# Lightning attention followed by a gated feed-forward: the five sums of w_out's quarters in tiles of their own, all formed by GpSimd, and the last products in column halves

## The chip, the cores and the metric

The kernel runs on 1 core of one Trainium2 chip. The metric is the device time of one execution in microseconds (us), lower is better. Times of a kernel are given as the median of several runs; a profile is one further execution, with its own time.

## The reference

Attention with a decay per head over blocks of 64 positions (batch 4, 8 heads, 768 positions, 64 channels), and then a feed-forward layer of 3072 tokens x 512 with a width of 2048 whose gate is h * cos(h):

```python
for b in range(nb):                      # 12 blocks of 64
    intra = np.einsum('bhic,bhjc->bhij', qb, kb) * Dmask[None]
    intra = np.einsum('bhij,bhjd->bhid', intra, vb)
    inter = np.einsum('bhid,bhde->bhie', qb * lam_pow[None], kv_state)
    out[:, :, sl] = intra + inter
    kb_dec = kb * rev_pow[None]
    kv_state = lam_block[None, :, None, None] * kv_state + np.einsum('bhsd,bhse->bhde', kb_dec, vb)
...
x = attn_out.transpose(0, 2, 1, 3).reshape(B * S, H * D)   # 3072 x 512
h = x @ w_in                             # 512 x 2048
g = h * np.cos(h)
return (g @ w_out).astype(np.float32)    # 2048 x 512
```

## The kernel before, in words

**Blocks and tiles.** The 3072 tokens are 24 blocks of 128 (n = 0 to 23), handled in pairs (pair p holds blocks 2p and 2p+1). The first two pairs ("spans") have code of their own at the start of the kernel (`add_span`). The feed-forward takes the blocks in nine tiles of 4, 2, 2, 2, 2, 4, 2, 2, 4 blocks (`TILES`, L32).

**Attention per pair.** `prepare` (L355) loads q, k and v of a pair over SP's DMA queue, scales q (L369) and v (L377) and casts k (L373), from pair 3 on all six on GpSimd, and from pair 3 on has q and k transposed by DMAs that SP issues (L405) into qkT. The loads of the next pair's q, k and v stand behind these two transposes on SP's queue. `add_scores` and `add_stretch` hold TensorE's part: scores (L447), the update of the state (L459), values (L509, L541); VectorE masks the scores (L452) and adds up the state (L465); ScalarE copies the outputs into xT (L549), the feed-forward's input.

**Feed-forward, plain tiles (0 to 4), `add_ffn`.** Hidden products (L1001), cosine on ScalarE (L1007), gate on VectorE (L1013), output products with w_out (L1048), copies and stores. The outputs of blocks 0 to 11 are held in the ring o_held until pair 10's transposes are issued, and stored by L1072 and L1074.

**Feed-forward, fast tiles (5 to 8, `FAST`), `add_fast_ffn`.** The product with w_out is done for two blocks at a time by one Strassen step: g is split by blocks and halves of the width, w_out into quarters 11, 12, 21, 22 (halves of its 2048 rows by halves of its 512 columns), and seven products replace eight. They need sums of g's parts, formed by VectorE per tile (L850, L852, L853, bf16), and five sums of w_out's quarters, formed once (`add_w_sums`, L776). The products (L897, numbered "1" to "7") go into PSUM banks A, B, C, for the last pair of blocks also D. ScalarE copies bank A (L914), VectorE forms the differences E (L921) and the outputs (L931 or L932, L958 or L959), which SP and, for the last piece, ScalarE's queue store (L948, L949, L964, L966).

**The five sums before.** 11+22, 12-22 and 21-11 (`WIDE`) are formed by GpSimd into three tiles of the ring "wide" (3 buffers), which before that hold s_m_sp0, s_m_sp1 and v_sp of the spans. Each is made in four instructions of 128x512 elements. Each of these twelve depends on the scaling of one block's v, from block 6 to block 17 (`SLOT`, L37), so that two stand in GpSimd's stream per pair. 21+22 and 11+12 are formed by VectorE, in eight instructions, in place: they overwrite the quarters 21 and 12 of w_out itself, so they also wait for the last output product of the plain tiles (`closed`) and for the GpSimd sums that read the same quarters.

**What sets the order.** All work is given as tasks with an engine, a duration, dependencies and a priority to a planner (`Planner.order`, L87). It simulates the engines in time, starts on each the task of lowest priority number among those that can start first, and the instructions are emitted in the order of the plan. Rings of buffers (`BUFS`) and the 8 PSUM banks are part of the simulation; a task with `lock` (VectorE's sums) and GpSimd's tasks are not planned at the same time. `SEQ` (L39) fixes the order of the products within a pair of blocks: for the last pair of blocks "5234176", each in two groups g of four of the eight slices of the width.

**The last pair of blocks.** Products "7" and then "6" are the last 16 instructions of TensorE (L897, 256 columns each). VectorE adds E to "7" (first L959), then to "6" (second L959); SP stores the first, ScalarE's queue the second.

Of the kernel before, what the change touches and what calls it, by code (L numbers as in the profile page):

```python
# [10 lines left out]
F32 = mybir.dt.float32  # L11
BF16 = mybir.dt.bfloat16
# [6 lines left out]
SPANS = 2  # L19
# [12 lines left out]
TILES = [4, 2, 2, 2, 2, 4, 2, 2, 4]  # L32
WIDE = ["11+22", "12-22", "21-11"]
CMB = (-4.0, 1.0, 6.0)
HASTE = 10.0
ON = ["DDDDDDDDDD"] * 9
SLOT = list(range(6, 18))  # L37
WSUM = [("11+22", "POOL", 2, 70.0), ("12-22", "POOL", 2, 70.0), ("21-11", "POOL", 2, 70.0), ("21+22", "DVE", 2, 100.0), ("11+12", "DVE", 2, 100.0)]
SEQ = [[(n, (g,)) for g, x in enumerate(("52341", "34521")) for n in x] + [(n, (0, 1)) for n in "76"], [(n, (0, 1)) for n in "5234176"]]  # L39
# [130 lines left out]
def kernel(  # L170
# [10 lines left out]
    nc = tc.nc  # L181
    B, H, S, D = q.shape
    P = 128
    NB = S // P
    NBLK = B * NB
    NP = H // 2
# [13 lines left out]

    BUFS = {"ld": 4, "qk": 3, "v_s": 6, "qkT": 3, "s_m": 4, "cos": 3, "o_held": 13, "cmb": 6, "SA": 1, "E": 1}
    ctx.enter_context(tc.manual_schedule())
# [6 lines left out]
    def bank(i, shape, dt, name):  # L209
# [405 lines left out]
    spans, span_deps = [], []  # L615
    span_s = [consts.tile([P, 2, NP, 2, P], BF16, tag="wide", bufs=3, name=f"s_m_sp{x}") for x in range(SPANS)]
    span_vs = consts.tile([P, SPANS, H, 2, D], BF16, tag="wide", bufs=3, name="v_sp")
    span_v = [span_vs[:, x] for x in range(SPANS)]
# [138 lines left out]

    W, w_sum, passed, closed = {}, {}, {}, [None]
# [12 lines left out]

# [19 lines left out]

    def right(what, f):
        a, z = what[:2], what[3:]
        if z:
            if what in WIDE:
                return W[what][:, f]
            return w_out_sb[:, f, high] if what == "11+12" else w_out_sb[:, HF + f, low]
        return w_out_sb[:, f + (HF if a[0] == "2" else 0), low if a[1] == "1" else high]

    def add_fast_ffn(i):  # L800
# [75 lines left out]
        for p in range(np_):  # L876
# [9 lines left out]
            for name, gs in SEQ[min(p, 1)]:  # L886
                to, half = where_[name]
                what = plan_of[name][2]
                for g in gs:
                    k += 1  # L890
                    opens = opening.get(name) if name not in count else None

                    def product(task, name=name, g=g, p=p, to=to, half=half, what=what, opens=opens):
# [3 lines left out]
                        return [nc.tensor.matmul(t, lhsT=left(name, f, p), rhs=right(what, f),  # L897
                                                 start=(f % QF == 0 and opens is not None), stop=(f == HF - 1), skip_group_check=True)
                                for f in range(QF * g, QF * g + QF)]
# [4 lines left out]
                    t.many = True  # L904
                    before = done[name] = t
                    count[name] = count.get(name, 0) + 1
# [45 lines left out]

            def second_out(_, half, cut=None, p=p):
                if ("o2", i, p) not in live:
                    live["o2", i, p] = work.tile([P, 2, HM], F32, tag="o_held", bufs=BUFS["o_held"], name="o_sb")
                o, e = live["o2", i, p], live["E", i, p]
                if half is None:
                    return nc.vector.tensor_add(o, live["f", i, p, "C"], e)  # L958
                return nc.vector.tensor_add(o[:, half], live["f", i, p, "CD"[half]][:, half], e[:, half])  # L959

            def store_second(_, half, p=p, rows=rows):
                o = live["o2", i, p]
                if half != 0:
                    nc.sync.dma_start(out=out[rows(0), low], in_=o[:, 1])  # L964
                if half != 1:
                    (nc.scalar if half == 0 else nc.sync).dma_start(out=out[rows(1), high], in_=o[:, 0])  # L966

            if last:
                x = pl.add("DVE", DUR["half"][0], [done["7"], done["e"]], partial(second_out, half=1), at(1.0), get="o_held", lat=DUR["half"][1])
                y = pl.add("DVE", DUR["half"][0], [done["6"], x], partial(second_out, half=0), at(1.0), lat=DUR["half"][1])  # L970
                x.frees = [dma("SP", 0.6, 0.7, partial(store_second, half=1), n0 + 2 * p + 9, [x], ordered=False)[1],
                           dma("ACT", 0.6, 0.7, partial(store_second, half=0), n0 + 2 * p + 9, [y], ordered=False)[1]]
                heads["C"].bank_frees, heads["D"].bank_frees = [[y]], [[x]]
                e0.frees = [x, y]
            else:
                x = pl.add("DVE", DUR["gate"][0], [done["7"], done["6"], done["e"]], partial(second_out, half=None), at(1.0), get="o_held", lat=DUR["gate"][1])
                x.frees = [dma("SP", 0.95, 1.3, partial(store_second, half=None), n0 + 2 * p + 9, [x], ordered=False)[1]]
                heads["C"].bank_frees = [[x]]
                e0.frees = [x]
# [3 lines left out]
    def add_ffn(i):  # L983
# [48 lines left out]
        for j in range(nb):  # L1032
# [5 lines left out]
            for piece, part in enumerate(pieces):  # L1038
# [21 lines left out]
                o_last[i] = store  # L1060
                closed[0] = store

# [158 lines left out]
```

## Time and profile before

| what | value |
|---|---|
| median of 3 runs | 200.58 us (200.28 to 203.41) |
| profiled execution, own time | 200.86 us |
| span of the profiled execution | 199.2 us |
| granted TensorE clock, mean | 0.999 |
| mean of a GpSimd sum of quarters (128x512, bf16) | 1.15 us, 12 of them |
| VectorE sums of quarters (128x512, bf16) | 0.41 to 1.07 us, 8 of them, 109.4 to 119.3 us after the start |

The engines are named PE (TensorE; PEld is its weight loads), DVE (VectorE), ACT (ScalarE), POOL (GpSimd) and SP (SyncE, which issues DMAs). In a row in order of time the first number is the start in us from the beginning of the span, the second the length; a row may hold several like instructions (x count); in brackets at its end stands the idle time of the engine ahead of it and who ended it. "issue" as the cause means that the profile shows nothing that the engine waited for. Busy times are modelled for matmuls, whose ends overlap, so a single product reads longer than the distance to the next.

### The profile page before, as it was taken

To read this page: it belongs to the slowest core of one execution; us is meant where nothing else is said; L and a number is where in the kernel's file an instruction comes from. 1 tells how busy PE (TensorE), PEld (TensorE's weight loads), DVE (VectorE), ACT (ScalarE), POOL (GpSimd) and SP (SyncE) were. 2 spreads that over 40 slices of the span, in tenths; PEclk is the share of its full clock that TensorE was granted. 3 is DMA by queue.
4 is the path that set the end of the run, shared out by engine and by line. 5 is a ranking of instruction groups with operands and counts; after the bars stand their busy time and mean duration, and the time that the engine had idled before them with its cause. 6 is when DMAs were issued, how large, how long until landed. Compare 5 with 4: busy or idle time off the path is not lost.

```text
span 199.2 us, 6216 instructions
## 1 busy us (share of the span) xinstructions
PE 190.0 (95%) x2577; PEld 130.1 (65%) x2599; DVE 146.3 (73%) x284; ACT 113.7 (57%) x217; POOL 79.3 (40%) x98
## 2 busy tenths in 40 slices
PE   8999999999999999999999998999799999999993
PEld 3577444658748647858655444778788885656882
DVE  2978772448857816957755899999797898599933
ACT  4888771329778636929564886544434565565110
POOL 5893002285856766778687373001640000000000
PEclk9999999999999999999999999999999999999999
DMA  5999999989999989899999999798991011001133
GB/s 161 306 190 203 206 203 240 318 192 159 248 188 170 216 175 221 166 255 149 250 188 285 186 238 125 174 379 240 226 177 56 3 54 56 0 4 49 56 105 107
DMA packets 98254, 34.48 MB, mean 173 GB/s; under 512 B 84914, under 2 KB 96178, under 8 KB 98226
## 3 DMA queue, kind: packets, MB, share of 16 engines
q1 hardware_dynamic: 91248, 29.76, 69.5%
q0 software_dynamic: 6832, 4.20, 14.5%
q8 instruction: 20, 0.33, 0.7%
q10 hardware_dynamic: 146, 0.13, 0.2%
q14 instruction: 8, 0.07, 0.1%
HBM read 27.26 MB, written 6.29 MB: 168 GB/s over the span
## 4 chain that ended last, share of the span: by engine, by line
PE 87%; DVE 7%; DMA 2%; issue 2%; ACT 1%; DVEq 0%
PE ps_h L1001 21%; PE ps_f L1048 21%; PE ps_h L820 17%; PE ps_f L897 17%; DVE g L829 3%; DMA sp_f<-in_q_dram 2%; DVE cmb L850 2%; PE ps_o L509 2%; PE ps_t L642 1%; PE ps_o L541 1%; PE ps_kv L459 1%; PE ps_s L447 1%; PE ps_s L653 1%; PE ps_o L679 1%; PE ps_idle L1143 1%
## 5 line engine op out<-in xcount | busy, mean ns | idle before, releaser
L826 ACT ACTIVATE cos<-ps_h,halfpi 128x512 f32<-128x512 f32 x48 | 32.9, 688 | 26.4 <-PE ps_h L820 24.9
L820 PE MATMUL ps_h<-xT,w_in_sb 128*128 128x256 bf16 (+1 forms) x251 | 46.6, 325 | 1.2 <-DVE g L829 0.9
L1013 DVE TENSOR_TENSOR g<-ps_h,cos 128x256 bf16<-128x256 f32 (+1 forms) x85 | 37.8, 459 | 12.2 <-ACT cos L1007 10.8
L1048 PE MATMUL ps_f<-w_out_sb,g 128*128 128x512 bf16 x177 | 42.3, 379 | 1.7 <-issue 1.3
L1001 PE MATMUL ps_h<-xT,w_in_sb 128*128 128x256 bf16 (+1 forms) x338 | 43.5, 286 | 0.1
L1007 ACT ACTIVATE cos<-ps_h,halfpi 128x256 f32<-128x256 f32 (+1 forms) x85 | 39.1, 505 | 7.1 <-PE ps_h L1001 6.9
L1001 PEld LDWEIGHTS <-w_in_sb 128*128 128x128 bf16 x340 | 33.0, 98 | 10.4 <-DMA w_in_sb<-in_moe_w_in_dram 0.3
L369 POOL TENSOR_TENSOR qk<-q_f,q_scale 128x512 bf16<-128x512 f32 x19 | 20.0, 1070 | 40.9 <-DMA q_f<-in_q_dram 37.5
L829 DVE TENSOR_TENSOR g<-ps_h,cos 128x512 bf16<-128x512 f32 x48 | 32.1, 685 | 5.3 <-ACT cos L826 5.2
L820 PEld LDWEIGHTS <-w_in_sb 128*128 128x128 bf16 x256 | 24.9, 98 | 14.4 <-DVE g L829 1.0
L1048 PEld LDWEIGHTS <-g 128*128 128x128 bf16 x192 | 18.0, 98 | 18.7
L377 POOL TENSOR_TENSOR v_s<-v_f,v_scale 128x512 bf16<-128x512 f32 x19 | 20.1, 1057 | 13.9 <-DMA v_f<-in_v_dram 11.8
L897 PEld LDWEIGHTS <-g 128*128 128x128 bf16 x192 | 18.6, 98 | 4.0
L549 ACT CAST xT<-ps_o 128x512 bf16<-128x512 f32 x15 | 8.1, 589 | 15.0 <-PE ps_o L541 12.6
L897 PEld LDWEIGHTS <-cmb 128*128 128x128 bf16 x144 | 14.0, 98 | 3.8 <-DVE cmb L850 0.7
L452 DVE TENSOR_TENSOR s_m<-ps_s,mask 128x512 bf16<-128x512 f32 x20 | 12.9, 685 | 2.8 <-PE ps_s L447 2.3
L373 POOL CAST qk<-k_f 128x512 bf16<-128x512 f32 x18 | 11.3, 625 | 7.4 <-DMA k_f<-in_k_dram 7.2
L850 DVE TENSOR_TENSOR cmb<-g 128x1024 bf16<-128x1024 bf16 (+1 forms) x24 | 13.9, 604 | 0.2
L897 PE MATMUL ps_f<-w_out_sb,cmb 128*128 128x256 bf16 x96 | 13.3, 273 | 0.4 <-DVE cmb L850 0.4
L897 PE MATMUL ps_f<-w_out_sb,g 128*128 128x256 bf16 x96 | 12.4, 273 | 0.0
L1065 ACT COPY o_sb<-ps_f 128x512 f32<-128x512 f32 x12 | 6.9, 588 | 6.9 <-PE ps_f L1048 6.9
L465 DVE TENSOR_TENSOR sum<-sum,ps_kv 128x512 f32<-128x512 f32 x15 | 10.2, 683 | 0.6
(100 smaller groups left out, 191.4 us busy)
## 6 DMA issues: line engine op xcount, KB each, us to landing
q_f<-in_q_dram SPq DMA_DIRECT2D x20, 256.0 KB, 3.5
k_f<-in_k_dram SPq DMA_DIRECT2D x20, 256.0 KB, 4.5
v_f<-in_v_dram SPq DMA_DIRECT2D x20, 256.0 KB, 5.1
out_dram<-o_sb SPq DMA_DIRECT2D x31, 128.0 KB, 2.0
out_dram<-o_sb SPq DMA_DIRECT2D x8, 256.0 KB, 3.0
w_out_sb<-in_moe_w_out_dram POOLq DMA_DIRECT2D x3, 512.0 KB, 13.6
sp_f<-in_q_dram SPq DMA_DIRECT2D x2, 512.0 KB, 4.8
sp_f<-in_k_dram SPq DMA_DIRECT2D x2, 512.0 KB, 5.4
```

Source lines behind the costliest of these rows:

```text
L369: return vec[e].tensor_mul(new_qk()[:, 0, :, s], live.pop(("q_f", 2 * pr + s)), q_scale[:, c, :].unsqueeze(2).to_broadcast([P, H, D]))
L377: return vec[e].tensor_mul(live["v_s", 2 * pr + s], live.pop(("v_f", 2 * pr + s)), v_scale[:, c, :].unsqueeze(2).to_broadcast([P, H, D]))
L452: return nc.vector.tensor_mul(t, live["s", pr][s], mask.unsqueeze(1).to_broadcast([P, H, D]))
L820: return [nc.tensor.matmul(t[:, x], lhsT=w_in_sb[:, kd, f * P:(f + 1) * P], rhs=live["xT", i][:, kd, :cols], start=(kd == 0), stop=(kd == ...
L826: return nc.scalar.activation(c, live["h", i, fs[0]], AF.Sin, bias=halfpi)
L829: return nc.vector.tensor_mul(g_tile()[:, fs[0]:fs[-1] + 1:HF, :cols], live.pop(("h", i, fs[0])), live.pop(("c", i, fs[0])))
L850: return v.tensor_add(c, *{"5": (a11, a12), "2": (a21, a22), "1": (a11, a22)}[name])
L897: return [nc.tensor.matmul(t, lhsT=left(name, f, p), rhs=right(what, f), start=(f % QF == 0 and opens is not None), stop=(f == HF - 1), sk ...
L1001: return [nc.tensor.matmul(t[:, :n], lhsT=w_in_sb[:, kd, f * P:(f + 1) * P], rhs=live["xT", i][:, kd, at], start=(kd == 0), stop=(kd == KD ...
L1007: nc.scalar.activation(c[:, :n], live["h", i, f, at.start][:, :n], AF.Sin, bias=halfpi)
L1013: return nc.vector.tensor_mul(live["g", i][:, f, at], live.pop(("h", i, f, at.start))[:, :n], live.pop(("c", i, f, at.start))[:, :n])
L1048: return [nc.tensor.matmul(live["f", i, j, piece][:, :width], lhsT=live["g", i][:, f, j * P:(j + 1) * P], rhs=w_out_sb[:, f, part], start= ...
```

## The change

It does four things.

1. All five sums get tiles of their own in the ring "wide", which grows from 3 buffers to 5, so w_out's quarters are no longer overwritten, and the waits for `closed` and for other sums are dropped.
2. All five are formed by GpSimd, in 20 instructions. The new `SLOT` ties three of them to the scalings of v in each of the pairs 3 to 8 (blocks 6, 6, 7; 8, 8, 9; and so on to 16, 16, 17) and two to block 18.
3. Room is made: qk goes from 3 buffers to 2, o_held from 13 to 12, mask_sp shares the buffer of E, kv_bd that of SA.
4. In the last pair of blocks product "6" is formed in two column halves: all eight slices of the width for columns 0 to 127, then all eight for 128 to 255, 16 products of 128 columns in place of 8 of 256. The second output is then added and stored in three parts: the 256 columns of "7" (SP), the first 128 of "6" (SP), the last 128 (ScalarE's queue).

```diff
-WIDE = ["11+22", "12-22", "21-11"]
...
-SLOT = list(range(6, 18))
-WSUM = [("11+22", "POOL", 2, 70.0), ("12-22", "POOL", 2, 70.0), ("21-11", "POOL", 2, 70.0), ("21+22", "DVE", 2, 100.0), ("11+12", "DVE", 2, 100.0)]
+SLOT = [6, 6, 7, 8, 8, 9, 10, 10, 11, 12, 12, 13, 14, 14, 15, 16, 16, 17, 18, 18]
+WSUM = [(x, "POOL", 2, 70.0) for x in ("11+22", "12-22", "21-11", "21+22", "11+12")]
...
-    BUFS = {"ld": 4, "qk": 3, "v_s": 6, "qkT": 3, "s_m": 4, "cos": 3, "o_held": 13, "cmb": 6, "SA": 1, "E": 1}
+    BUFS = {"ld": 4, "qk": 2, "v_s": 6, "qkT": 3, "s_m": 4, "cos": 3, "o_held": 12, "cmb": 6, "SA": 1, "E": 1}
...
-    mask_sp = consts.tile([P, 2, P], F32)
+    mask_sp = work.tile([P, 2, P], F32, tag="E", bufs=BUFS["E"], name="mask_sp")
...
-    kv_bd = consts.tile([P, 2, NP, P], BF16)
+    kv_bd = work.tile([P, 2, NP, P], BF16, tag="SA", bufs=BUFS["SA"], name="kv_bd")
...
         def place(name, g):
-            if name in WIDE:
-                if name not in W:
-                    W[name] = consts.tile([P, HF, HM], BF16, tag="wide", bufs=3, name=f"w_{name}")
-                return W[name][:, QF * g:QF * g + QF]
-            return w_out_sb[:, QF * g:QF * g + QF, high] if name == "11+12" else w_out_sb[:, HF + QF * g:HF + QF * g + QF, low]
+            if name not in W:
+                W[name] = consts.tile([P, HF, HM], BF16, tag="wide", bufs=5, name=f"w_{name}")
+            return W[name][:, QF * g:QF * g + QF]
...
-                    t = pl.add(e, {"DVE": 0.07 + 0.55 / parts, "POOL": 2.08 / parts}[e], loaded + slot + (wide_free if name in WIDE else [closed[0]] + w_sum[{"11+12": "12-22", "21+22": "21-11"}[name], g]),
+                    t = pl.add(e, {"DVE": 0.07 + 0.55 / parts, "POOL": 2.08 / parts}[e], loaded + slot + wide_free,
...
+                        if last and name == "6":
+                            m = slice(g * P, (g + 1) * P)
+                            return [nc.tensor.matmul(t[:, m], lhsT=left(name, f, p), rhs=right(what, f)[:, m],
+                                                     start=False, stop=(f == HF - 1), skip_group_check=True) for f in range(HF)]
...
             if last:
-                x = pl.add("DVE", DUR["half"][0], [done["7"], done["e"]], partial(second_out, half=1), at(1.0), get="o_held", lat=DUR["half"][1])
-                y = pl.add("DVE", DUR["half"][0], [done["6"], x], partial(second_out, half=0), at(1.0), lat=DUR["half"][1])
...
+                parts = [slice(HM, DM), slice(0, P), slice(P, HM)]
+                x = second(parts[0], [done["7"]], True, at(1.0))
+                y = second(parts[1], [done["6", 0], x], False, at(1.0))
+                z = second(parts[2], [done["6", 1], y], False, at(1.0))
+                x.frees = [second_store(parts[0], nc.sync, [x], 0.6), second_store(parts[1], nc.sync, [y], 0.4), second_store(parts[2], nc.scalar, [z], 0.4)]
```

`second(at, ...)` is one VectorE addition over the columns `at`, `second_store` the store of the same columns. The rest of the diff carries these through.

More of the change, by code (lines that the diff above doesn't have):

```diff
@@ L615 @@
     spans, span_deps = [], []
-    span_s = [consts.tile([P, 2, NP, 2, P], BF16, tag="wide", bufs=3, name=f"s_m_sp{x}") for x in range(SPANS)]
-    span_vs = consts.tile([P, SPANS, H, 2, D], BF16, tag="wide", bufs=3, name="v_sp")
+    span_s = [consts.tile([P, 2, NP, 2, P], BF16, tag="wide", bufs=5, name=f"s_m_sp{x}") for x in range(SPANS)]
+    span_vs = consts.tile([P, SPANS, H, 2, D], BF16, tag="wide", bufs=5, name="v_sp")
     span_v = [span_vs[:, x] for x in range(SPANS)]
@@ L756 @@
     hid, closing = [], None
-    W, w_sum, passed, closed = {}, {}, {}, [None]
+    W, w_sum, passed = {}, {}, {}
     low, high = slice(0, HM), slice(HM, DM)
@@ L794, in right @@
         if z:
-            if what in WIDE:
-                return W[what][:, f]
-            return w_out_sb[:, f, high] if what == "11+12" else w_out_sb[:, HF + f, low]
+            return W[what][:, f]
         return w_out_sb[:, f + (HF if a[0] == "2" else 0), low if a[1] == "1" else high]
@@ L891, in add_fast_ffn, with product @@
                     opens = opening.get(name) if name not in count else None
-                    def product(task, name=name, g=g, p=p, to=to, half=half, what=what, opens=opens):
+                    def product(task, name=name, g=g, p=p, to=to, half=half, what=what, opens=opens, last=last):
                         if opens:
@@ L904, in add_fast_ffn @@
                     t.many = True
-                    before = done[name] = t
+                    before = done[name] = done[name, g] = t
                     count[name] = count.get(name, 0) + 1
@@ L951, in add_fast_ffn, with second_out @@
             out1.frees = [dma("SP", 0.95, 1.3, store_first, n0 + 2 * p + 8, [done["o1", 0]], ordered=False)[1]]
-            def second_out(_, half, cut=None, p=p):
+            def second_out(_, at, p=p):
                 if ("o2", i, p) not in live:
[L955 to L959, printed above, removed]
@@ L961, in store_second @@
-            def store_second(_, half, p=p, rows=rows):
-                o = live["o2", i, p]
[L963 to L966, printed above, removed]
-            if last:
-                x = pl.add("DVE", DUR["half"][0], [done["7"], done["e"]], partial(second_out, half=1), at(1.0), get="o_held", lat=DUR["half"][1])
-                y = pl.add("DVE", DUR["half"][0], [done["6"], x], partial(second_out, half=0), at(1.0), lat=DUR["half"][1])
[L971 to L974, printed above, removed]
-            else:
-                x = pl.add("DVE", DUR["gate"][0], [done["7"], done["6"], done["e"]], partial(second_out, half=None), at(1.0), get="o_held", lat=DUR["gate"][1])
-                x.frees = [dma("SP", 0.95, 1.3, partial(store_second, half=None), n0 + 2 * p + 9, [x], ordered=False)[1]]
@@ new lines, in second_out, with store_second @@
+                    live["o2", i, p] = work.tile([P, DM], F32, tag="o_held", bufs=BUFS["o_held"], name="o_sb")
+                t = live["f", i, p, "D" if last and at.start == HM else "C"].rearrange("p a m -> p (a m)")
+                return nc.vector.tensor_add(live["o2", i, p][:, at], t[:, at], live["E", i, p].rearrange("p a m -> p (a m)")[:, at])
+            def store_second(_, at, queue, p=p, rows=rows):
+                o = live["o2", i, p]
+                if at.stop > HM:
+                    nc.sync.dma_start(out=out[rows(0), low], in_=o[:, high])
+                if at.start < HM:
+                    e = min(at.stop, HM)
+                    queue.dma_start(out=out[rows(1), HM + at.start:HM + e], in_=o[:, at.start:e])
@@ new lines, in second, with second_store @@
+            def second(at, deps, get, prio):
+                n = (at.stop - at.start) / 256.0
+                return pl.add("DVE", 0.07 + 0.265 * n, deps + [done["e"]], partial(second_out, at=at), prio, get="o_held" if get else None, lat=0.17)
+            def second_store(at, queue, deps, us):
+                return dma("SP" if queue is nc.sync else "ACT", us, 1.5 * us, partial(store_second, at=at, queue=queue), n0 + 2 * p + 9, deps, ordered=False)[1]
+            if last:
+                parts = [slice(HM, DM), slice(0, P), slice(P, HM)]
[3 more added lines that the diff above has]
+                x.frees = [second_store(parts[0], nc.sync, [x], 0.6), second_store(parts[1], nc.sync, [y], 0.4), second_store(parts[2], nc.scalar, [z], 0.4)]
+                heads["C"].bank_frees, heads["D"].bank_frees = [[z]], [[x]]
+                e0.frees = [x, y, z]
+            else:
+                x = second(slice(0, DM), [done["7"], done["6"]], True, at(1.0))
+                x.frees = [second_store(slice(0, DM), nc.sync, [x], 0.95)]
@@ L1060, in add_ffn @@
                 o_last[i] = store
-                closed[0] = store
                 def project_out(_, eng, j=j, piece=piece, width=width, tag=tag):
```

## The prediction

> **What bounds the kernel now.** I read the page first, then busy time by stretch, then each engine in order of time around the weakest stretch.
>
> ```profile
> span 199.2 us, 6216 instructions
> PE 190.0 (95%) x2577; PEld 130.1 (65%) x2599; DVE 146.3 (73%) x284; ACT 113.7 (57%) x217; POOL 79.3 (40%) x98
> ```
>
> TensorE (PE) works in 190.0 of 199.2 us, so all that an edit can win by better order is inside the other 9.2 us. Where these are is shown by busy time per stretch (columns: stretch, length, busy time and instructions of PE, weight loads, VectorE = DVE, ScalarE = ACT, GpSimd = POOL, then clock, DMA share, GB/s):
>
> ```profile
> 109.00:120.00 11.00, 10.95 (x169) 5.51 (x170) 10.28 (x19) 8.82 (x14) 6.57 (x7) 1.00 1.38 212
> 120.00:133.00 13.00, 11.61 (x96) 8.15 (x95) 12.97 (x21) 6.72 (x11) 1.17 (x2) 1.00 0.76 210
> ```
>
> From 120 to 133 TensorE misses 1.39 us and VectorE works without a break (12.97 of 13). One stretch earlier VectorE is almost as full, but TensorE misses only 0.05. TensorE in order of time shows the two places (the bracket is the idle time before, and who ended it):
>
> ```profile
> 121.19 4.49 PE L820 MATMUL ps_h<-xT,w_in_sb 128*128 128x512 bf16 x19 [0.93 <-DVE g L829]
> ...
> 132.20 0.61 PE L897 MATMUL ps_f<-w_out_sb,cmb 128*128 128x256 bf16 x4 [0.41 <-DVE cmb L850]
> ```
>
> Both waits, 0.93 + 0.41 = 1.34 us, are for VectorE. What VectorE does ahead of them, with the last ScalarE cosine of that run, the one GpSimd scaling that lies beside, and the group of the VectorE sums from the costliest groups by form:
>
> ```profile
> 109.38 1.07 DVE L776 TENSOR_TENSOR w_out_sb<-w_out_sb 128x512 bf16<-128x512 bf16 x1
> ...
> 119.35 1.05 DVE L776 TENSOR_TENSOR w_out_sb<-w_out_sb 128x512 bf16<-128x512 bf16 x1
> 120.44 1.29 DVE L829 TENSOR_TENSOR g<-ps_h,cos 128x512 bf16<-128x512 f32 x2
> 121.64 1.28 DVE L452 TENSOR_TENSOR s_m<-ps_s,mask 128x512 bf16<-128x512 f32 x2
> 122.84 1.50 DVE L850 TENSOR_TENSOR cmb<-g 128x1024 bf16<-128x1024 bf16 x1
> ...
> 131.46 1.28 DVE L850 TENSOR_TENSOR cmb<-g 128x1024 bf16<-128x1024 bf16 x2
> ```
>
> ```profile
> 118.89 0.69 ACT L826 ACTIVATE cos<-ps_h,halfpi 128x512 f32<-128x512 f32 x1 [0.18 <-PE ps_h L820]
> ```
>
> ```profile
> 122.75 1.04 POOL L377 TENSOR_TENSOR v_s<-v_f,v_scale 128x512 bf16<-128x512 f32 x1 [2.63 <-DMA v_f<-in_v_dram]
> ```
>
> ```profile
> L776 DVE TENSOR_TENSOR w_out_sb<-w_out_sb 128x512 bf16<-128x512 bf16 x8 | 4.9, 634 | 0.0
> ```
>
> The eight sums that VectorE forms stand in 109.4 to 120.4, among the gates of the first Strassen tile (tile 5), and push the last two gates to 120.44. The second of these two needs only the cosine that ends at 118.89 + 0.69 = 119.58.
>
> **The change part by part.**
>
> *Sums leave VectorE.* Eight instructions, 4.9 us, go. The last two gates then start when their cosines end, the second at about 119.6 instead of 121.0 (120.44 plus half of 1.29). VectorE is some 1.3 us earlier from there on, and the bank for which TensorE waited until 121.19 is free by 120.3, when the attention products in front are just through (121.19 - 0.93 = 120.26). Term: -0.93. The second wait, 0.41 at 132.20, ends on a row of VectorE work with no gap from 119.35 on. That row starts 1.3 us earlier and TensorE comes only 0.93 earlier, so 0.4 of it is covered; besides, the sum that took 1.50 at 122.84 beside GpSimd's scaling at 122.75 has the chance to run ahead of it. Term: -0.41. Bounds for the two: both gone, -1.34; none, because TensorE stalls at the next thing, 0.
>
> *Sums go to GpSimd.* What a sum costs there, and how GpSimd's rounds are spaced now: a round per pair of blocks is two scalings of q (L369), two casts of k, two scalings of v, with now two sums behind them; the bracket is GpSimd's idle time ahead of the round.
>
> ```profile
> 52.62 2.04 POOL L369 TENSOR_TENSOR qk<-q_f,q_scale 128x512 bf16<-128x512 f32 x2 [0.62 <-DMA q_f<-in_q_dram]
> ...
> 64.18 2.04 POOL L369 TENSOR_TENSOR qk<-q_f,q_scale 128x512 bf16<-128x512 f32 x2 [1.58 <-PE ps_h L1001]
> ...
> 75.06 2.04 POOL L369 TENSOR_TENSOR qk<-q_f,q_scale 128x512 bf16<-128x512 f32 x2 [1.68 <-PE ps_s L447]
> ...
> 85.33 2.04 POOL L369 TENSOR_TENSOR qk<-q_f,q_scale 128x512 bf16<-128x512 f32 x2 [0.32 <-DMA q_f<-in_q_dram]
> ...
> 91.08 1.16 POOL L776 TENSOR_TENSOR w_21-11_2005<-w_out_sb 128x512 bf16<-128x512 bf16 x1
> ...
> 96.11 2.04 POOL L369 TENSOR_TENSOR qk<-q_f,q_scale 128x512 bf16<-128x512 f32 x2 [1.75 <-DMA q_f<-in_q_dram]
> ...
> 105.30 2.04 POOL L369 TENSOR_TENSOR qk<-q_f,q_scale 128x512 bf16<-128x512 f32 x2 [0.86 <-DMA q_f<-in_q_dram]
> ...
> 114.78 2.10 POOL L369 TENSOR_TENSOR qk<-q_f,q_scale 128x512 bf16<-128x512 f32 x2 [2.55 <-DMA q_f<-in_q_dram]
> ```
>
> The new SLOT puts three sums instead of two behind the v's of pairs 3 to 8 (one more, 1.15 us each) and two behind block 18 (2.3 us where there was none): 6 x 1.15 + 2 x 1.15 = 9.2 us. Against the idle times in order (pairs 4 to 10) the rounds start late by 0.53, 0, 0, 0.83, 0, 0.29, 0. If no lateness is made up, pair 8 is late by 0.53 + 0.83 = 1.36 us and pair 10 by 1.65. Queued behind a late q scaling are the k casts, then on SP's queue the two DMA transposes of that pair, and behind these the loads of the next q, k and v. TensorE is met at the scores (L447). For pairs 7 and 8: issues of the transposes, time to landing of the second, and the scores in the chain that ended last:
>
> ```profile
> L405 SPq DMA_TRANSPOSE qkT<-qk x2: 1255/2350/3446, 87.4 to 90.9; - x2
> ...
> qkT<-qk SPq DMA_TRANSPOSE x1, 4.5
> ```
>
> ```profile
> L405 SPq DMA_TRANSPOSE qkT<-qk x2: 1362/1482/1603, 98.2 to 100.3; - x2
> ...
> qkT<-qk SPq DMA_TRANSPOSE x1, 4.1
> ```
>
> ```profile
> 97.84 0.26 PE ps_s L447 x32
> 98.10 0.32 PE ps_kv L459 x32
> ...
> 106.45 0.26 PE ps_s L447 x32
> ```
>
> Pair 7 lands at 90.9 + 4.5 = 95.4 for 97.84, pair 8 at 100.3 + 4.1 = 104.4 for 106.45: 2.4 and 2.05 us to spare. A lateness of 1.36 stays inside. Term: 0; with that cover gone it costs what exceeds 2.05. One sum also moves ahead of a second v scaling at pairs 7 and 9 (priorities 70 to 74 against those of the v's); for pair 7 that is until 91.08 + 2 x 1.15 + 1.04 (the row of 122.75) = 94.4 at the earliest, with 1.36 of lateness 95.8, and its state update starts at 98.10.
>
> *Homes.* qk loses one buffer of three. The first q scaling of pair p then waits for the state update of pair p-2 instead of p-3; the closest is pair 9, 105.30 against 98.10 + 0.32, 6.9 us apart. o_held goes from 13 to 12 buffers; the first Strassen output then waits for the first held block's store:
>
> ```profile
> 122.58 5.94 SPq L1072 DMA_DIRECT2D out_dram<-o_sb  x8
> ```
>
> ```profile
> 133.86 0.68 DVE L931 TENSOR_TENSOR o_sb<-ps_f,SA 128x512 f32<-128x512 f32 x1
> ```
>
> 11.3 us lie between. mask_sp and kv_bd give way to tiles written after 130 us. All of this: 0.
>
> *Last products in column halves.* The end, as it is, with the nearest rows for 128 wide products (L399, in the chain that ended last) and their weight loads, and what the DMA moved from 195 to 200 us in steps of 0.125 us:
>
> ```profile
> 194.06 1.91 PE L897 MATMUL ps_f<-w_out_sb,g 128*128 128x256 bf16 x16
> 195.13 0.42 DVE L959 TENSOR_TENSOR o_sb<-ps_f,E 128x256 f32<-128x256 f32 x1
> ...
> 196.00 0.42 DVE L959 TENSOR_TENSOR o_sb<-ps_f,E 128x256 f32<-128x256 f32 x1 [0.45 <-PE ps_f L897]
> 196.46 0.38 ACTq L966 DMA_DIRECT2D out_dram<-o_sb  x1
> ```
>
> ```profile
> 34.98 0.45 PE ps_t L399 x8
> ```
>
> ```profile
> 34.60 0.65 PEld L399 LDWEIGHTS <-qk 128*128 128x128 bf16 x8
> ```
>
> ```profile
> GB/s 123 344 377 172 33 16 279 385 328 41 0 156 377 393 123 0 0 0 57 328 393 254 17 0 0 0 0 0 0 0 0 0 0 0 0 0 0 0 0 0
> ```
>
> Today product "6" is 8 instructions of 256 columns, one each 1.75/16 = 0.109 us, 0.87 in all. In halves it is 16 of 128 columns, each with its own weight load. In the chain that ended last the eight products of L399 hold 0.45 us, 0.056 each; but their weights were loaded ahead, behind longer products, and the eight loads take 0.65, or 0.08 each. Sixteen in a row can't stay ahead: I take 16 x 0.08 = 1.28, +0.41 us; by 0.056 it is 0.90, +0.03.
>
> On this the Trainium skill speaks against the change: "TensorE: Matmul & The Clock Gate", section "Back-to-back issue gap", gives about 81 ns for each product of 128 columns in a stream of loads and products, against 56 for a product by itself. By its figure 16 products are 1.30 us and the end is 0.43 later, by the isolated one 0.03; the row of loads sides with the former.
>
> The last VectorE sum shrinks from 256 to 128 columns. By 0.42 for 256 and 0.68 for 512 (L931) that is 0.26 per 256 and 0.29 for 128: -0.13. The last store, 128 KB, shows as the burst 57 to 254 of the row above, about 0.4 us; half of it: -0.17 (bounds 0 and -0.2). End: +0.41 - 0.13 - 0.17 = +0.1, between -0.3 and +0.4.
>
> **Sum.** -0.93 - 0.41 + 0 + 0 + 0.1 = -1.24 us on the profiled execution of 200.86 us, whose span is 199.2: 199.6. The median of the three runs is 200.58, 0.28 lower, so 199.3. The likeliest case by itself: from -1.34 - 0.3 (198.9) to -0.93 + 0.4 (200.1).
>
> **Rivals.**
>
> *The gap only moves.* At 120.3 the banks of the scores, the state update and the outputs of pair 9 are still full, and TensorE lives on the two that gates free. If ScalarE's copies or the scores' masking then end the wait, the 1.34 comes back and the end's +0.1 is left: 200.7. For it: 12.97 of 13 us of VectorE leaves little air. Against it: without the sums that load is 1.3 us ahead.
>
> *GpSimd late (slower).* The q loads are issued behind the transposes, which wait for GpSimd. If the loads' landing moves along, the idle time ahead of a round is no reserve and each of the five rounds of pairs 3 to 7 adds 1.15: 5.75 at pair 8's scores. Beyond 2.05 TensorE has no xT to go on with: +3.7 there, on top of -1.24: 203.0. It decides from a lateness of 2.05 at pair 8. For it: 0.32 ahead of pair 7, SP's queue in one line. Against it: the sums lie between k casts and the next q, beside transposes and load, and 1.75 ahead of pair 8 takes one.
>
> *A third gap goes too.* One wait has no named cause:
>
> ```profile
> 141.66 0.22 PE L541 MATMUL ps_o<-qkT,S 64*64 64x64 bf16 x2 [1.04 <-issue]
> ```
>
> If it hangs on what the transfers do at that moment, a shift may undo it: -1.04, 198.3. Nothing shows that it should.
>
> **How the numbers follow.** Forecast 0.60, gap moves 0.17, GpSimd late 0.15, third gap 0.08. Range 198.2 to 201.6: it holds the forecast, the third gap, the moved gap and the mild part of a late GpSimd, and leaves out its full price. A change of 2%, 4.0 us, is about what a measurement of this kernel can tell from none. Faster than that would need over three times the two gaps: 0.01. Slower needs more than a late GpSimd at full price (203.0 against 204.6): 0.04. Within 2%: 0.95.
>
> **What would show it.** Right: no L776 on VectorE, twenty on GpSimd (about 23 us); the waits for L829 near 120 and L850 near 131 gone, PE idle in that stretch under 0.5; scores of pairs 4 to 9 without a wait on transposes; the last 16 products 1.2 to 1.3 us, the last VectorE sum 0.29. Wrong: TensorE idle ahead of L447 between 50 and 110, a wait of the same size for another releaser at 120 to 133, or 0.9 us for the 16 products.

## The result and the profile after

| kernel | median | range | runs |
|---|---|---|---|
| before | 200.37 us | 199.79 to 203.41 | 10 |
| changed | 199.12 us | 198.70 to 199.71 | 10 |

The ratio is 0.9942 (95%: 0.9925 to 0.996): 1.25 us less, within the 2% that count as no difference here, but clear of 1. Ratios here and below are formed without disturbed runs, so they need not equal the quotient of two medians.

The profiled execution of the changed kernel took 198.72 us with a span of 197.0, against 200.86 and 199.2 before. The two spans differ by 2.2 us, the medians by 1.25: the profile of before happened to lie 0.49 above its kernel's median, that of after 0.40 below. The experiments show what part of the 2.2 belongs to the change.

The page's first lines, and busy time in the same two stretches as before (columns as in the prediction):

```profile
span 197.0 us, 6257 instructions
PE 192.0 (97%) x2607; PEld 130.4 (66%) x2607; DVE 142.3 (72%) x277; ACT 113.6 (58%) x217; POOL 87.3 (44%) x106
```

```profile
109.00:120.00 11.00, 11.00 (x128) 5.22 (x126) 7.84 (x14) 9.26 (x15) 7.33 (x8) 1.00 0.99 219
120.00:133.00 13.00, 13.00 (x162) 9.77 (x149) 13.00 (x23) 7.06 (x13) 0.00 (x0) 1.00 0.79 243
```

From 109 to 120 VectorE falls from 10.28 to 7.84 us. From 120 to 133 it is as full as before, 13.00 of 13, and yet TensorE has no idle time: it is not VectorE's load in the stretch that decided but how early it entered it. TensorE around the place of the two waits, in order of time, and VectorE beside it:

```profile
120.16 0.51 PE L540 MATMUL ps_o<-qkT,S 64*64 64x64 bf16 x32
120.60 4.49 PE L815 MATMUL ps_h<-xT,w_in_sb 128*128 128x512 bf16 x20
124.93 0.60 PE L896 MATMUL ps_f<-w_out_sb,cmb 128*128 128x256 bf16 x4
...
132.79 0.60 PE L896 MATMUL ps_f<-w_out_sb,cmb 128*128 128x256 bf16 x4
```

```profile
119.67 0.16 DVE L525 COPY spare<-ps_o 1x1 f32<-1x1 f32 x1
119.86 1.29 DVE L824 TENSOR_TENSOR g<-ps_h,cos 128x512 bf16<-128x512 f32 x2
121.06 1.28 DVE L451 TENSOR_TENSOR s_m<-ps_s,mask 128x512 bf16<-128x512 f32 x2
122.26 0.68 DVE L845 TENSOR_TENSOR cmb<-g 128x1024 bf16<-128x1024 bf16 x1
```

No bracket stands behind the products: both waits are gone (the profile lists no stop under 0.15 us). The margin is small, though. Before, TensorE went on at 121.19, 0.75 behind the start of the first of the two gates (120.44), as in all five profiles with such a wait; the second ended only at 121.73, so it was not the one waited for. Now 119.86 + 0.75 = 120.61, and TensorE goes on at 120.60, just in time.

What kept that gate back was one sum, not all eight. In both kernels the gates stand behind a small copy of TensorE's outputs (L525, before L526). Now they follow the copy at once; before, the sum of 119.35 to 120.40 stood between them. The copy before, and what GpSimd did beside the sum:

```profile
119.16 0.16 DVE L526 COPY spare<-ps_o 1x1 f32<-1x1 f32 x1
```

```profile
119.08 1.04 POOL L377 TENSOR_TENSOR v_s<-v_f,v_scale 128x512 bf16<-128x512 f32 x1 [0.15 <-POOL qk L373]
```

Such a sum takes 0.41 us by itself. In the fourteen profiles of this case none of the 237 VectorE additions of its form (128x512, bf16) without a GpSimd instruction beside it took over 0.43 us; with one beside it they took up to 1.29, this one 1.05. The same holds for the sum of g's parts behind the gates (L845, before L850): 0.68 in place of 1.50, with no scaling by GpSimd beside it in this execution (1.02 in the second profile of the changed kernel, where one is).

GpSimd's sums (instruction counts, min/median/max in ns, first and last start) and its rounds (q scalings of pairs 3, 7, 8 and 10), with the first round of before for comparison:

```profile
L773 POOL TENSOR_TENSOR w_11+22_953<-w_out_sb x4: 1152/1154/1157, 48.3 to 58.0; 128x512 bf16<-128x512 bf16 x4
...
L773 POOL TENSOR_TENSOR w_11+12_2331<-w_out_sb x4: 1152/1156/1158, 99.8 to 108.9; 128x512 bf16<-128x512 bf16 x4
```

```profile
42.26 2.04 POOL L368 TENSOR_TENSOR qk<-q_f,q_scale 128x512 bf16<-128x512 f32 x2
...
82.23 2.04 POOL L368 TENSOR_TENSOR qk<-q_f,q_scale 128x512 bf16<-128x512 f32 x2
...
91.61 2.04 POOL L368 TENSOR_TENSOR qk<-q_f,q_scale 128x512 bf16<-128x512 f32 x2
...
111.98 2.04 POOL L368 TENSOR_TENSOR qk<-q_f,q_scale 128x512 bf16<-128x512 f32 x2 [0.95 <-DMA q_f<-in_q_dram]
```

```profile
42.37 2.04 POOL L369 TENSOR_TENSOR qk<-q_f,q_scale 128x512 bf16<-128x512 f32 x2
```

From pair 3 to pair 10 the rounds took 111.98 - 42.26 = 69.7 us, before 114.78 - 42.37 = 72.4 (71.5 and 74.8 in a second profile of each). GpSimd comes to most rounds without idle time, and none is late; pair 8 starts at 91.61 (before 96.11).

The end: product "6" with its weight loads, and VectorE and the last store behind it.

```profile
192.62 0.99 PEld L894 LDWEIGHTS <-g 128*128 128x128 bf16 x16
192.73 1.06 PE L894 MATMUL ps_f<-w_11+12_2331,g 128*128 128x128 bf16 x16
193.01 0.42 DVE L956 TENSOR_TENSOR o_sb<-ps_f,E 128x256 f32<-128x256 f32 x1 [0.20 <-PE ps_f L896]
...
193.83 0.49 DVE L956 TENSOR_TENSOR o_sb<-ps_f,E 128x128 f32<-128x128 f32 x2 [0.39 <-PE ps_f L894]
...
194.35 0.38 ACTq L964 DMA_DIRECT2D out_dram<-o_sb  x1
```

From the first product of "6" to the end of the span it is 197.0 - 192.73 = 4.27 us, before 199.2 - (194.06 + 0.87) = 4.27 (the page gives spans to 0.1 us, so such figures are good to 0.05). VectorE's two halves stand in one row, back to back from 193.83 on: the first half's sum did not begin when its own eight products were through, at about 193.3 (192.73 + half of 1.06), but behind all sixteen.

One more row, in the place of the third gap (1.04 at 141.66 before):

```profile
138.57 1.22 PE L815 MATMUL ps_h<-xT,w_in_sb 128*128 128x256 bf16 x8
```

There is no stop in this execution, only 0.18 more than the 1.04 that eight such products take elsewhere.

### The profile page after: what moved, and what is told of

Its sections match the earlier page's. It is cut to its first block, busy times and chain, and to the rows that moved or that the text cites. A ratio compares the mean times of both kernels' runs of the same rounds, so it can differ in the third digit from the quotient of the medians.

```text
span 197.0 us, 6257 instructions
## 1 busy us (share of the span) xinstructions
PE 192.0 (97%) x2607; PEld 130.4 (66%) x2607; DVE 142.3 (72%) x277; ACT 113.6 (58%) x217; POOL 87.3 (44%) x106
## 4 chain that ended last, share of the span: by engine, by line
PE 89%; DMA 6%; SPq 1%; POOL 1%; ACT 1%; issue 0%; DVE 0%; DVEq 0%; POOLq 0%
PE ps_f L1054 22%; PE ps_h L815 21%; PE ps_h L1007 20%; PE ps_f L896 18%; DMA sp_f<-in_k_dram 3%; DMA w_in_sb<-in_moe_w_in_dram 3%; PE ps_kv L458 2%; PE ps_o L508 2%; PE ps_o L540 2%; PE ps_s L446 1%; SPq L277 1%; POOL k_sp L633 1%; PE ps_f L894 0%; PE ps_t L398 0%; ACT cos L821 0%; PE ps_kv L737 0%
## 5 line engine op out<-in xcount | busy, mean ns | idle before, releaser
L815 PE MATMUL ps_h<-xT,w_in_sb 128*128 128x512 bf16 (+1 forms) x256 | 47.0, 326 | 0.0
L1054 PE MATMUL ps_f<-w_out_sb,g 128*128 128x512 bf16 x192 | 44.8, 379 | 0.0
L1007 PE MATMUL ps_h<-xT,w_in_sb 128*128 128x256 bf16 (+1 forms) x340 | 43.8, 286 | 0.1
L815 PEld LDWEIGHTS <-w_in_sb 128*128 128x128 bf16 x256 | 24.8, 98 | 13.7 <-issue 0.3
L1054 PEld LDWEIGHTS <-g 128*128 128x128 bf16 x192 | 18.0, 98 | 18.7
L896 PEld LDWEIGHTS <-g 128*128 128x128 bf16 x184 | 17.9, 98 | 3.9
L896 PEld LDWEIGHTS <-cmb 128*128 128x128 bf16 x144 | 14.0, 98 | 3.1
L845 DVE TENSOR_TENSOR cmb<-g 128x1024 bf16<-128x1024 bf16 (+1 forms) x24 | 13.4, 584 | 0.2
L896 PE MATMUL ps_f<-w_out_sb,cmb 128*128 128x256 bf16 x96 | 13.4, 273 | 0.0
L468 ACT CAST S<-sum 128x512 bf16<-128x512 f32 x15 | 9.1, 620 | 2.0 <-DVE sum L464 2.0
```

The costliest lines, as they stand in the source:

```text
L815: return [nc.tensor.matmul(t[:, x], lhsT=w_in_sb[:, kd, f * P:(f + 1) * P], rhs=live["xT", i][:, kd, :cols], start=(kd == 0), stop=(kd == ...
L845: return v.tensor_add(c, *{"5": (a11, a12), "2": (a21, a22), "1": (a11, a22)}[name])
L1007: return [nc.tensor.matmul(t[:, :n], lhsT=w_in_sb[:, kd, f * P:(f + 1) * P], rhs=live["xT", i][:, kd, at], start=(kd == 0), stop=(kd == KD ...
L1054: return [nc.tensor.matmul(live["f", i, j, piece][:, :width], lhsT=live["g", i][:, f, j * P:(j + 1) * P], rhs=w_out_sb[:, f, part], start= ...
```

## The experiments

The theory: the gain is VectorE's sums having left the stretch ahead of 120, GpSimd's extra sums are free, and the column halves are worth nothing. The rivals: the halves carry part of the gain; GpSimd's sums cost something that hides part of the gain; the third gap is part of it. In the table, 0 means no stop of 0.15 us or more.

| kernel | ratio to before, 95% | TensorE waits for VectorE, 118 to 135 us | third gap | "6" to end |
|---|---|---|---|---|
| before (first profile) | 1 | 1.34 | 1.04 | 4.27 |
| before again (e1) | | 1.52 | 0.46 | 4.20 |
| halves alone (e2) | 1.0008 (0.997 to 1.0045) | 1.95 | 0.49 | 4.23 |
| changed, without halves (e3) | 0.9968 (0.994 to 0.9996) | 0 | 0.67 | 4.45 |
| the same again (e12) | 0.9951 (0.9928 to 0.9974) | 0 | 1.22 | 4.46 |
| changed, two sums on VectorE (e4) | 0.999 (0.9954 to 1.0025) | 2.32 | 0.53 | 4.21 |
| the same again (e11) | 0.9984 (0.9955 to 1.0013) | 0.88 | 0.95 | 4.26 |
| changed (first profile) | 0.9942 (0.9925 to 0.996) | 0 | 0 | 4.27 |
| changed again (e5) | 0.9938 (0.9915 to 0.9962) | 0 | 0.66 | 4.37 |
| changed, eight sums left out (e6) | 0.9937 (0.9911 to 0.9964) | 0 | 1.15 | 4.28 |
| changed, three banks (e8) | 0.996 (0.9938 to 0.9982) | 0.32 | 0.33 | 4.66 |

**The kernel before once more** (no edit).

> The kernel before once more, unchanged, for a second profile. Both waits of TensorE for VectorE (0.93 us ahead of the hidden products near 121, 0.41 us near 132) belong to the program and should return within 0.1 us each. The wait of 1.04 us at 140.6 that the first profile ends with 'issue': if it belongs to the program it returns with about 1 us at the same products; if it was that one execution's, it is gone or smaller and the span is up to 1 us under 199.2. GpSimd's rounds of pairs 3 to 10: if their spacing (72.4 us from pair 3's first q scaling to pair 10's) belongs to the program it returns within 0.5 us.

It took 201.64 us. Its waits for VectorE:

```profile
121.34 0.44 PE L459 MATMUL ps_kv<-v_s,qk 64*64 64x64 bf16 x31 [0.90 <-DVE g L829]
...
122.82 4.49 PE L820 MATMUL ps_h<-xT,w_in_sb 128*128 128x512 bf16 x19 [0.62 <-DVE g L829]
```

Two waits of 0.90 and 0.62, in other places than in the first profile, with nothing near 132. So the places and sizes are those of one execution; that VectorE's gates hold TensorE there is not. The rounds took 74.8 us against the 72.4 expected: they vary by execution too.

**The column halves alone.** The kernel before with the last part of the change:

```diff
+                        if last and name == "6":
+                            m = slice(g * P, (g + 1) * P)
...
+                parts = [slice(HM, DM), slice(0, P), slice(P, HM)]
```

> The kernel before with the column halves of the last products alone. Theory (the gain is VectorE's relief, the end gives nothing): 200.4 us, within 0.2 of before, the part behind the start of product '7' as long as before (5.1 us to the end of the span). Rival (the halves carry the gain): 199.1 us.

200.61 us, no difference; the waits for VectorE stay, 1.26 + 0.69 = 1.95.

**The changed kernel without the halves**, twice, the second time to narrow the first:

```diff
-                        if last and name == "6":
-                            m = slice(g * P, (g + 1) * P)
...
-                parts = [slice(HM, DM), slice(0, P), slice(P, HM)]
```

> The changed kernel with the last products as they were. Theory (VectorE's relief is the gain): 199.1 us, all the gain stays. Rival (the halves carry it): 200.3 us.

> The changed kernel with the end of the kernel before (product "6" whole, two stores) once more, on another chip, to narrow what the column halves are worth. If the whole gain comes from VectorE's sums having left, the ratio to the kernel before is 0.994 as for the changed kernel (0.9925 to 0.996), about 199.5 us, and the first look's 0.9968 was the low side of chance. If the halves carry a share of it, the ratio stays at 0.997, 0.5 us above the changed kernel. In both, no TensorE wait for VectorE between 118 and 135, and 4.2 to 4.45 us from the start of product "6" to the end of the span.

199.98 and 199.45 us. No wait for VectorE in either. The mean of the ratios is 0.996 (half the root of the squared half-widths: 0.0018 either way), that of the changed kernel's two 0.994 (0.0015). The difference of 0.2%, 0.4 us, has an uncertainty of 0.0023, so that a share of the halves between nothing and 0.9 us stays open from times alone. The profiles bound it closer. The end of the second:

```profile
193.94 1.04 PE L892 MATMUL ps_f<-w_11+12_2331,g 128*128 128x256 bf16 x8
194.22 0.42 DVE L954 TENSOR_TENSOR o_sb<-ps_f,E 128x256 f32<-128x256 f32 x1 [0.20 <-PE ps_f L892]
...
195.01 0.42 DVE L954 TENSOR_TENSOR o_sb<-ps_f,E 128x256 f32<-128x256 f32 x1 [0.36 <-PE ps_f L892]
195.47 0.38 ACTq L961 DMA_DIRECT2D out_dram<-o_sb  x1
```

From "6" to the issue of the last store it is 1.53 us whole and 1.62 in halves; from there to the end of the span 2.93 here and 2.74 before, 2.65 in halves. Over all profiles, three banks aside, "6" to the end is 4.20 to 4.46 whole (four profiles) and 4.18 to 4.39 in halves (nine): no gain of the halves shows.

**Two of the sums back on VectorE**, twice. Homes and halves stay; GpSimd forms twelve:

```diff
+SLOT = list(range(6, 18))
+WSUM = [(x, "POOL", 2, 70.0) for x in ("11+22", "12-22", "21-11")] + [("21+22", "DVE", 2, 100.0), ("11+12", "DVE", 2, 100.0)]
```

> The changed kernel, homes and column halves in place, but the sums 21+22 and 11+12 formed by VectorE again, at the same place as before (behind the last plain output product), and twelve sums on GpSimd. Theory (VectorE's eight instructions between 109 and 120 are the cause of the two waits): 200.3 us, both waits of TensorE for VectorE near 121 and 132 return with about 0.9 and 0.4 us. Rival (the homes, or the order that the planner makes with them, carry the gain): 199.1 us and no such waits.

> The changed kernel with 21+22 and 11+12 on VectorE again, once more, on another chip. VectorE's relief as the cause: 0.9 to 1.5 us above the changed kernel's 0.994 of before, so within 0.3 us of before, with both waits of TensorE for VectorE between 119 and 123.

```profile
121.38 0.44 PE L458 MATMUL ps_kv<-v_s,qk 64*64 64x64 bf16 x31 [1.49 <-DVE g L824]
...
123.14 4.49 PE L815 MATMUL ps_h<-xT,w_in_sb 128*128 128x512 bf16 x19 [0.83 <-DVE g L824]
```

200.44 and 200.43 us. The waits are back, 1.49 + 0.83 here, a single one of 0.88 in the second (at 121.57, where two were expected), and with them most of the time: the mean ratio is 0.9987 (0.0023), 0.0047 above the changed kernel's (0.0027), or 0.9 us of 200, between 0.4 and 1.5. This is the part that the removal of VectorE's sums, with the order that the plan makes without them, is shown to bring.

**The changed kernel again, and with eight sums left out** (the products that need them read two other sums):

```diff
+SLOT = list(range(6, 18))
+WSUM = [(x, "POOL", 2, 70.0) for x in ("11+22", "12-22", "21-11")]
...
+            return W[{"21+22": "12-22", "11+12": "21-11"}.get(what, what)][:, f]
```

> The changed kernel once more, unchanged, beside the kernels of this call. Ratio to the kernel before 0.994 if the gain holds on another chip. TensorE without a wait for VectorE near 121 and 132. If the quicker GpSimd rounds of its first profile (69.7 us from pair 3's first q scaling to pair 10's, against 72.4 before) belong to the program they return within 0.5; if they were that execution's, 72 to 75 as in the other kernels. The stop of TensorE that the profiles end with 'issue' near 141: none if it went with the change, 0.5 or more if it comes and goes by execution.

> Leaves out part of the computation: the sums 21+22 and 11+12 are formed by no engine (the products that need them read 12-22 and 21-11 instead), twelve sums stay on GpSimd at the old two per pair. Theory (GpSimd's eight more sums cost nothing): the same time as the changed kernel of this call within 0.3 us. Rival (GpSimd late, in part): faster than the changed kernel by 0.5 us or more.

199.50 and 199.65 us on the same chip, ratios 0.9938 and 0.9937. Nobody forms the eight sums in the second, and it isn't faster: on GpSimd they cost nothing that shows. By the spread of the two sets of runs (means of 199.53 and 199.58, the difference good to some 0.5 us) a hidden cost of more than 0.5 us is ruled out, a smaller one is not. In e5 the rounds took 71.5 us from pair 3 to pair 10, neither of the two values expected, and the third gap is back with 0.66.

**Sixteen more sums on GpSimd.** Four of the five sums are formed twice, 36 in place of 20:

```diff
+SLOT = [6, 6, 6, 7, 7, 8, 8, 8, 9, 9, 10, 10, 10, 11, 11, 12, 12, 12, 13, 13, 14, 14, 14, 15, 15, 16, 16, 16, 17, 17, 18, 18, 18, 18]
+WSUM = [(x, "POOL", 2, 70.0) for x in ("11+22", "11+22", "12-22", "12-22", "21-11", "21-11", "21+22", "21+22", "11+12")]
```

> The changed kernel with four of the five sums formed twice, so that GpSimd has 36 of them, five and six in a round where the changed kernel has three: 18.4 us more. A round then needs about 5.4 for q, k and v and 5.8 to 6.9 for sums, 11 to 12 us against a spacing of 9.5 to 11. Rival of the prediction (from 2.05 us of lateness at pair 8 TensorE stops): the rounds come 5 to 8 us late by pair 8, TensorE waits ahead of the values or scores of pairs 7 to 9, and the time is 3 to 6 us above the changed kernel. If transposes and loads have far more to spare than the 2.05 us: under 1 us above.

205.55 us, ratio 1.0239 (1.0212 to 1.0267): 6 us above the changed kernel on the same chip. GpSimd's round of pair 10 and where TensorE stopped:

```profile
120.50 2.50 POOL L368 TENSOR_TENSOR qk<-q_f,q_scale 128x512 bf16<-128x512 f32 x2
```

```profile
107.52 1.02 PE L1054 MATMUL ps_f<-w_out_sb,g 128*128 128x512 bf16 x4 [0.30 <-DMA qkT<-qk]
...
111.08 10.52 PE L815 MATMUL ps_h<-xT,w_in_sb 128*128 128x512 bf16 x47 [1.21 <-ACT xT L548]
...
138.30 0.19 PE L458 MATMUL ps_kv<-v_s,qk 64*64 64x64 bf16 x1 [1.91 <-DVE s_m L451]
```

The round is 8.5 us later than in the first profile of the changed kernel (111.98) and 6.4 later than in the second (114.07), and TensorE now waits for the transposes and for xT behind them, then for masks. The three stops shown are 3.4 of the 6 us; the rest was not taken apart. The order is another one, too: the plan reckons with the longer rounds and puts pair 7's scores behind 340 loads of w_in, not 328. So the slower rival's chain (GpSimd, transposes, scores, xT) exists, and its time comes when the reserve is used up: it is not used up by 9.2 us of sums, and it is by another 16 x 1.15 = 18.4.

**Three banks at the end.** In the changed kernel the two column halves of the last pair's products "3" and "6" go to PSUM banks of their own (product "3" is split by columns for that, and so is VectorE's addition for the first block):

```diff
+                            live["f", i, p, "F"] = bank(task.bank[1], [P, 2, HM], F32, "ps_f2")
...
+                            u = live["f", i, p, "CF"[g]][:, half]
```

> The changed kernel with the two column halves of the last pair's products '3' and '6' in PSUM banks of their own. In the changed kernel's profile the addition for the first half of '6' starts only when all 16 products are through (193.83, with the second half's behind it), though its own eight end 0.45 us earlier. If that is because both halves lie in one bank, the first addition now starts some 0.4 us ahead of the second, the second starts right behind the last product, and the end is 0.2 us earlier than in the changed kernel. If it is for another reason, the two additions still run back to back behind the last product and the time is the same.

```profile
193.64 1.06 PE L897 MATMUL ps_f<-w_11+12_2331,g 128*128 128x128 bf16 x16
...
193.93 0.65 DVE L968 TENSOR_TENSOR o_sb<-ps_f,E 128x256 f32<-128x256 f32 x2 [0.20 <-PE ps_f L903]
...
194.73 0.29 DVE L968 TENSOR_TENSOR o_sb<-ps_f,E 128x128 f32<-128x128 f32 x1 [0.16 <-PE ps_f L897]
```

The first row of VectorE holds the 256 columns of "7" and the first 128 of "6" (0.65 in place of 0.42): the first half's sum now runs while the second half is multiplied. From "6" to the end of VectorE it is 194.73 + 0.29 - 193.64 = 1.38 us, in the changed kernel 193.83 + 0.49 - 192.73 = 1.59: 0.21 less, about what was expected if sharing a bank is what held the first half back. The time shows nothing of it: 199.73 us, and the span ends 3.2 us behind the issue of the last store in place of 2.65. Why that is longer here is not settled.

**The third gap.** Two kernels move everything in TensorE's stream. In the first, twenty small products in place of one long one among the idle products of the first microseconds make the stream 36 instructions longer ahead of the gap; in the second, five idle products are left out, 14 instructions fewer:

```diff
-    ones_of(4 * P, F32)
+    for _ in range(20):
+        ones_of(64)
```

```diff
-    ones_of(4 * P, F32)
...
-            if now:
-                keep_awake(t.start - now, slow)
```

> The changed kernel with 20 small idle products of TensorE near 3.4 us in place of one long one, so that all that follows stands 36 instructions later in TensorE's stream. In the profiles so far the stop that ends with 'issue' near 141 lies at the same place of TensorE's instruction order in the kernel before (ahead of the last two L541) and in the changed one (ahead of the last two of eight hidden products), rows 4015 in both, though the work there differs: a place in the stream, not a piece of work. Theory (the next block of instructions comes late): the stop is now 36 instructions earlier in the work, ahead of the last four of the carried values (L540) of pair 10, and not at the hidden products; its size is 0.3 to 2 us. Rival (it belongs to the work, or to the transfers beside it): it stays ahead of the last two hidden products.

> The changed kernel without five idle products of TensorE in the first 10 us (they only keep it busy), so that all that follows stands 14 instructions earlier in its stream. Theory (the next block of instructions comes late): the place is now among the products of '3' behind the hidden ones, 0.6 to 0.9 us later in time, and the stop is smaller by that much or gone; the time is 0 to 0.6 us below the changed kernel, less what the first 15 us lose. Rival (it belongs to the work): a stop of 0.3 us or more stays ahead of the last two hidden products.

The stop in the changed kernel (second execution), with 36 instructions more, and with 14 fewer:

```profile
140.10 0.39 PE L815 MATMUL ps_h<-xT,w_in_sb 128*128 128x256 bf16 x2 [0.66 <-issue]
```

```profile
139.29 0.22 PE L540 MATMUL ps_o<-qkT,S 64*64 64x64 bf16 x4 [0.74 <-issue]
```

```profile
143.35 0.50 PE L896 MATMUL ps_f<-w_12-22_1277,g 128*128 128x256 bf16 x3 [0.41 <-issue]
```

The order there is L540 (32 products), eight of L896, eight of L815, eight of L896, each product with its weight load. In the changed kernel the stop stands ahead of the last two of L815. With 36 instructions more it stands 18 products earlier (6 of L815, 8 of L896, 4 of L540: "x4"); with 14 fewer, 7 later (2 and 5, 3 left: "x3"). In all twelve profiles that have the stop, exactly 2020 of TensorE's weight loads stand ahead of it. It is bound to a place in the stream, counted in instructions, and to none of the operations there. The kernel before has it at the same place, where L541 stands: in the changed kernel the plan runs that pair's attention 2.9 us earlier (136.38 in place of 139.29), which is why L815 stands there now. The page of every kernel lists a queue for the loading of code:

```profile
q8 instruction: 20, 0.33, 0.7%
```

20 packets in 0.33 MB are 16 KB each. The packet records of the traces bear on it: in each of the twelve profiles one packet of this queue ends 1.1 to 1.5 us before TensorE goes on (before 140.22 for 141.66; in the three rows above 138.60 for 140.10, 138.18 for 139.29, 142.03 for 143.35). In the first profile of the changed kernel it ends at 138.07, early enough but for the 0.18. So the reading is that the next block of TensorE's instructions comes late there. Right ahead stands the attention of a pair, some 250 instructions in 1.3 us, which uses a block up fast. The Trainium skill ("Runtime: NRT & Kernel Launch", section "Instruction fetch mechanics") states such blocks of 256 instructions, fetched ahead, and calls the cost of a block's boundary mostly hidden; here up to 1.22 us of it were not. The size, 0 to 1.22 in the executions of the table, goes with the time at which that packet comes; why it comes sooner or later stays open. Neither kernel is faster than before: 200.50 us (ratio 0.9994), and 202.34 (199.13 to 204.08, a wide scatter; ratio 0.9996, 0.9945 to 1.0047). In their profiles the first loses 1.1 us in the first 20 us, in a wait for w_in at 16.40. The second loses 3 us there, and hardly by waiting: without the idle products the same work takes TensorE longer (the first twelve hidden products 2.18 us at 16.80, in the changed kernel 1.50 at 14.09). No gain from a smaller stop could show beside that.

## Why the prediction was right

The forecast was 1.24 us less, and 1.25 was measured. Some of that agreement is luck, as the terms show.

**The two waits (-1.34).** Right in mechanism: they are there in every kernel with sums on VectorE (0.88 to 2.32) and gone without, but for 0.32 once. The sizes were one execution's, and so was the second place: no other profile has a wait near 132, and where a second wait came it stood near 121, ahead of the state update. What the removal brings is 0.9 (0.4 to 1.5) by the experiments, so that it may be all of the 1.25 or a part. The forecast had VectorE just in time (bank free at 120.3, TensorE there at 120.26), and so it came, by another way: it named the second of the two gates and let it start at 119.6, when its cosine ends; but TensorE goes on behind the first, and the gates start at 119.86, behind the small copy (L525) of TensorE's own outputs. Nor did all 4.9 us of sums matter, but those right ahead of the gates waited for. Where the sum between copy and gates takes 0.53, 0.60, 0.81, 1.02 and 1.05 us (e1, e2, e4, e11, before), the wait ahead of the hidden products is 0.62, 0.69, 0.83, 0.88 and 0.93; the wait ahead of the state update (e1, e2, e4) is for a gate right behind two more sums, of 1.15 to 1.94 us together. The 0.32 of a wait that is back in e8 is for a gate right behind a sum of g's parts that took 1.32 us, in the first profile of the changed kernel 0.69: with a margin of nothing, one slow addition brings a wait back.

**GpSimd (0).** Right, and by more than the working: the forecast let 1.15 us more per round make pair 8 late by 1.36 us. In the changed kernel's two profiles no round came more than 0.4 us later than in the first profile of before, and pair 8's came 4.5 and 2.8 us sooner. The idle time ahead of a round in one profile was not the whole reserve; the spacing of the rounds differs by up to 2.4 us between two executions of the same kernel (72.4 and 74.8). The 2.05 us at which the rival would decide was never reached, and e7 shows what is behind it.

**Homes (0).** Not tested alone; the two runs with homes and halves but two sums on VectorE (0.999 and 0.9984) leave no room for a loss of more than some 0.2 us from the two together.

**The end (+0.1).** The total is 0.0, with three terms mis-sized. The products: not +0.41 but 1.10 - 1.07 = +0.03 up to the last addition (193.83 - 192.73 against 196.00 - 194.93). Sixteen loads took 0.99 us, 0.062 each: a row of eight loads that ran at 0.08 elsewhere was no bound. The sixteen products took 1.06 as a row, or 0.9 by the forecast's own reckoning, which takes 0.16 off a row for the last product's end; 0.9 is what the forecast named as a sign of being wrong, and for this term it was. The Trainium skill's 81 ns in a stream ("TensorE: Matmul & The Clock Gate", section "Back-to-back issue gap"), on whose side the forecast came down, does not hold here; the 56 ns of a product by itself do. VectorE: not -0.13 but +0.07 (0.49 for two halves against 0.42), since the halves share a bank and the first waits for the second. The store: not -0.17 but -0.09 (2.65 against 2.74), and in both forms some profiles are 0.1 to 0.2 longer (2.92 and 2.93 of four whole, 2.76 and 2.78 of nine in halves).

**The third gap.** Rightly left out of the sum. It belongs to the execution and to a place in the stream, not to the change; that it was nearly absent in the profile of after is why the spans differ by more than the medians. Counted by TensorE's weight loads from the start, the changed profile is 0.4 us late against that of before when the first wait comes, 0.6 us early after it, 1.3 after the second, 2.3 after the third gap and 2.2 at the end. So it wins 1.0, 0.7 and 1.0 us at the three stops, where the brackets say 0.93, 0.41 and 1.04, and had lost 0.4 us before them.

## What to carry to other kernels

Where two engines meet, work taken off the late one pays only as far as the early one waits: 4.9 us left VectorE, 9.2 came to GpSimd, and what counted was about 1 us of TensorE's wait, made by the sums that stood right ahead of the gates it waited for. Such a wait is one execution's number: look at a second profile before its size goes into a sum. And the column split at the end gained nothing here: up to the issue of the last store it lost 0.09 us, and the smaller store gave about as much back.

## What the runs showed of the hardware

- A stop of TensorE at a fixed place of its instruction stream, 0 to 1.22 us by execution, that 36 instructions more or 14 fewer ahead of it move by as many, and that ends 1.1 to 1.5 us behind the end of a 16 KB packet of the queue that loads code.
- VectorE additions in bf16 (128x512) of 0.41 to 0.43 us by themselves, and of up to 1.29 with a GpSimd instruction beside them.
- A VectorE read of one half of a PSUM bank that started only when TensorE's products into the other half were done (193.83 for 193.3); in a bank of its own it ran beside them. Whether a wait of the program or the bank itself held it was not told apart.
- Sixteen products of 128 columns with a weight load each in 1.06 us, where eight of 256 columns take 1.04.
